# Four edits to the opening of an mLSTM cell with a SwiGLU block: who asks for a load, how a weight block is converted, which engine rounds it, and in what order

## The chip, the cores and the metric

The kernel runs on one core of a Trainium2 chip. The metric is the device time of one execution in microseconds (us), as a median of several runs. The core has a matrix engine (TensorE, PE in the profile; PEld is its weight load), VectorE (DVE), ScalarE (ACT), GpSimd (POOL) and SyncE (SP), which issues transfers. Each engine works through its own list of instructions in order, and semaphores make one wait for another. Transfers (DMAs) are asked for by SP, by ScalarE or by GpSimd.

## The reference

Two stages follow each other. The first is an mLSTM cell over 4 batches, 8 heads, 768 steps and a head size of 40:

```
m_new  = max(f + m, i);  f_stab = exp(f + m - m_new);  i_stab = exp(i - m_new)
C = f_stab * C + i_stab * v k^T;   n = f_stab * n + i_stab * k
y = sigmoid(o) * (C q) / max(|n.q|, 1)
```

Its output, as 3072 tokens of 320 features, goes through a SwiGLU block with d_ff = 1536: `(silu(x @ w_gate) * (x @ w_val)) @ w_out`. The inputs q, k, v and the gates are float32; the three weight matrices are float64 (`np.random.randn` scaled), so that every weight arrives as two 32-bit words.

## The kernel before

The 768 steps are cut into 6 groups of 128. For each group the cell is computed in its parallel form (scores, a matrix of decay weights, a carried state), its result is turned into `xT`, and the 512 tokens of the group go through the SwiGLU block. Group 0 differs from the others: while it runs, the weights are still arriving and have to be turned from float64 into float32 on the chip. The whole change lies in this stretch, up to about 51 us.

**Weights.** The gate and value matrices are cut into 12 blocks of 128 columns (`NFC`), the output matrix into 6 further blocks (numbers 12 to 17). `piece_load` (L166) asks for them in pieces: pieces 0 to 3 are blocks 0 to 3, piece 4 is blocks 4 and 5, piece 5 blocks 6 and 7, and so on. A piece has three parts: part 0, called GATE, is the gate matrix (partitions 0 to 63), parts 1 and 2, called VALUE, are the value matrix (partitions 64 to 127). Part 0 is asked for by SP, parts 1 and 2 by GpSimd (L200).

**Conversion.** A block is converted in three steps. `scale` (L221) has ScalarE make two tiles, `top` from the high words (L226) and `low` from the low words (L228). `join` (L231) has VectorE make the float's bits from `top` (L235, L236). `rounded` (L240) adds `low` as a whole number: on GpSimd, or on VectorE if it is told so (both L243). `top` has one buffer and `low` has two, so the next `scale` waits for the `join` before it. `portion` (L245) scales only some of a block's five chunks of the contraction. Block 0 is converted in two portions, chunks 0 to 1 and 2 to 4; block 1 at once, and both, like block 2, are rounded by VectorE. After that the list `on_vector` (L1041) names the blocks that VectorE rounds: 9 and 10.

**Blocks of group 0.** `hidden(0, m)` (L751) multiplies block m with `xT` in TensorE (L759), ten matmuls into two PSUM banks, which the profile shows as 20 records. The banks come from a ring of four, so block m takes those of block m - 2. Then `first` is run, which converts the block that `ahead` names (block 3 at m = 1, block 4 at m = 2, block 5 at m = 3, ...), and only then follow the SiLU on ScalarE (L764) and the multiplication on VectorE (L765), which release the two banks. After each `hidden`, the entries of `slots` for that m are run.

**Gates of the later groups.** Between the blocks VectorE computes the cell's decay terms for groups 1 to 5. `late_sums` (slot 1) is a running sum of the forget gates (L326) and a subtraction from the input gates (L328), with a memset by GpSimd (L327). `late_maxima` (slot 2) is two small copies (L331, L332) and a running maximum `M_sb` (L333), which GpSimd then stores to memory (`M_store`, L343). From there SP loads it back, broadcast, as `w_sb` (`weights_load`, L515, slot 3). `late_decay` follows in slot 3, the reading of `w_sb` (`weights_cap`, L530) in slot 6.

**The queue of SP around block 0.** SP asks for q, k, v, then for the output gates of the first group (`o_sb`, L139), then for the GATE parts of pieces 0 and 1 (called at L674), 2, 3, 4 and 5. ScalarE's sigmoid of the output gates (L540) comes before the first group's result is turned (`seam`, L507 and the copies at L143) and before block 0 is scaled. GpSimd asks for the VALUE part of piece 0 at L679, between the two calls of `first_values` (L591), multiplies the gates in (`first_gate`, L629) and asks for the other VALUE parts in between.

Of the kernel before, what the change touches and what calls it, by code (L numbers as in the profile page):

```python
# [14 lines left out]
ALU = mybir.AluOpType  # L15
# [9 lines left out]
def kernel(  # L25
# [18 lines left out]
    nc = tc.nc  # L44
# [13 lines left out]
    NKC = DM // HP  # L58
# [15 lines left out]
    def flat(t):  # L74
        return t.rearrange("p c t -> p (c t)")
# [32 lines left out]
    k_sb = const.tile([128, BH, DP], F32)  # L108
# [54 lines left out]

    homes = {}

    def piece_load(p, home=None, parts=(0, 1, 2)):  # L166
        kind, m, n = PIECES[p]
        if kind == "gv":
            a, d = NKC, n * 128
            gate_w, val_w = (w[:, m * 128:(m + n) * 128].rearrange("(c p) f -> p c f", p=HP) for w in (moe_w_gate, moe_w_val))  # L170
            src = [(slice(0, HP), slice(0, NKC), gate_w), (slice(HP, 128), slice(0, NKC - 1), val_w[:, 1:]),
                   (slice(HP, 128), slice(NKC - 1, NKC), val_w[:, 0:1])]
        else:
            a, d = n, DM
            src = [(slice(0, 128), slice(0, n), moe_w_out[m * 128:(m + n) * 128].rearrange("(a p) d -> p a d", p=128))]
        if src[0][2].dtype == F32:
            for r, cs, w in [src[x] for x in parts if x < len(src)]:
                if kind == "o":
                    nc.sync.dma_start(out=wo_sb[r, m:m + n, :], in_=w)
                else:  # L180
                    for x in range(n):
                        nc.sync.dma_start(out=wgv_sb[r, m + x, cs], in_=w[:, :, ts(x, 128)])
            return
        if p in homes:
            raw = homes[p]
        else:
            if p < 4:
                if p == 0:
                    homes["raw"] = conv.tile([128, 4 * NKC * 128], U32, name="raw")
                base = homes["raw"] if p < 2 else raw_h.rearrange("p m t -> p (m t)").bitcast(U32)  # L190
                raw = base[:, ds(2 * (p % 2) * a * d, 2 * a * d)]
            elif home is None:
                raw = conv.tile([128, 4 * NKC * 128], U32, name="raw")
            else:
                raw = home.rearrange("p a t -> p (a t)").bitcast(U32)
            raw = homes[p] = raw[:, 0:2 * a * d]
        for x in parts:
            if x < len(src):
                r, cs, w = src[x]
                eng = nc.gpsimd if x else nc.sync  # L200
                eng.dma_start(out=raw[r].rearrange("p (a d) -> p a d", a=a)[:, cs], in_=w.bitcast(U32))
        words = raw.rearrange("p (a d two) -> p a d two", two=2, a=a)
        raws[p] = (words[:, :, :, 0], words[:, :, :, 1])
        split(p)


    blocks = {}
# [23 lines left out]
    def join(j):  # L231
        if j in blocks:
            lo, top, dst = blocks[j]
            both = dst.bitcast(U32)
            nc.vector.tensor_scalar(both, top, scalar1=3, scalar2=None, op0=ALU.logical_shift_left)  # L235
            nc.vector.scalar_tensor_tensor(both, in0=top, scalar=0x80000000, in1=both, op0=ALU.bitwise_and,  # L236
                                           op1=ALU.bitwise_or)
            blocks[j] = (lo, dst.bitcast(I32))

    def rounded(j, eng=None):  # L240
        if j in blocks:
            lo, dst = blocks.pop(j)
            (eng or nc.gpsimd).tensor_tensor(dst, dst, lo, op=ALU.add)  # L243

    def portion(j, c):  # L245
        if j not in blocks:
            return
        lo, hi, dst = blocks[j]
        if ("room", j) not in homes:
            homes["room", j] = [conv.tile([128, NKC * 128], t, name=n, bufs=x).rearrange("p (a d) -> p a d", a=NKC)  # L250
                                for t, n, x in ((F32, "top", 1), (I32, "low", 2))]
        top, low = homes["room", j]
        nc.scalar.mul(top[:, c], hi[:, c].bitcast(F32), 2.0 ** -112)
        nc.scalar.mul(low[:, c], lo[:, c], 2.0 ** -29)
        blocks[j, c.start] = (low[:, c], top[:, c].bitcast(U32), dst[:, c])

    def convert(j, eng=None):
        scale(j)
        join(j)
        rounded(j, eng)  # L260
# [63 lines left out]

    def late_sums():
        nc.vector.tensor_tensor_scan(flat(f_sb), flat(keep1), flat(f_sb), 0.0, op0=ALU.mult, op1=ALU.add)  # L326
        nc.gpsimd.memset(step1, 0.0)  # L327
        nc.vector.tensor_sub(i_sb, i_sb, f_sb)  # L328

    def late_maxima():  # L330
        nc.vector.tensor_copy(step1[:, 0:1, 0:1], f0[0:BH, end].unsqueeze(1))  # L331
# [258 lines left out]
    def first_values(P):  # L590
        nc.gpsimd.tensor_tensor(vw_sb[:, heads(P)], v_sb[:, heads(P)], w_end[:, heads(P)].to_broadcast([128, UH, D1]),  # L591
                                op=ALU.mult)
# [15 lines left out]
    def first_own(u):  # L608
        both = bank("first_y", "gen")
        spare_of["y", u] = both[:, H * D1:]  # L610
        first_y[u] = both[:, 0:H * D1].rearrange("p (h d) -> p h d", d=D1)
        for h in range(H):
            for i in range(2):
                nc.tensor.matmul(first_y[u][half(i), h, :], lhsT=W0[:, u * H + h, half(i)], rhs=v_sb[:, u * H + h, :],
                                 start=True, stop=True)

    def first_x(u):
        y = first_y.pop(u)
        den = work.tile([128, UH, 1], F32, name="den")[:, 0:H]
        nc.vector.tensor_scalar(den, y[:, :, D:], scalar1=1.0, scalar2=None, op0=ALU.max)  # L620
        nc.vector.scalar_tensor_tensor(den, in0=y[:, :, D:], scalar=-1.0, in1=den, op0=ALU.mult, op1=ALU.max)
        nc.vector.reciprocal(den, den)
        nc.vector.tensor_tensor(x_sb[:, u, 0:DM].rearrange("p (h d) -> p h d", d=D), y[:, :, 0:D],
                                den.to_broadcast([128, H, D]), op=ALU.mult)
# [46 lines left out]
    spread(G, 3, k_sb, 1)  # L671
    first_exp(1)
    first_scores(0)
    for p in range(2):  # L674
        piece_load(p, parts=GATE)
    turn_one(1, q_sb, qT, (A, A), "gen")
    first_ends(1)
    first_values(0)
    piece_load(0, parts=VALUE)  # L679
    first_own(0)  # L680
    turn_one(1, k_sb, kT, (A, A), "gen")
    nc.scalar.activation(warm, warm, AF.Sigmoid)
    first_values(1)
    first_x(0)
    first_own(1)
    first_x(1)
# [25 lines left out]
    join((0, 2))  # L712
    rounded((0, 2), V)
    fill("add", 6, False)
    convert(1, V)
    nc.scalar.activation(warm, warm, AF.Silu)
    first_kept(0, ps0, A)
    first_kept(1, ps1, A)
# [315 lines left out]
    def load_all(dst, a, n, eng=nc.sync):  # L1034
# [3 lines left out]
    run = lambda f, *a, **b: (lambda: f(*a, **b))  # L1038


    on_vector = (9, 10)  # L1041
    ahead = {0: [], 1: [3], 2: [4], 3: [5], 4: [6], 5: [7], 6: [8], 7: [9], 8: [10], 9: [], 10: [], 11: []}
    slots = {
        0: [run(piece_load, 5), run(piece_load, 6, wo_sb)],
        1: [run(late_sums)],
        2: [run(late_maxima), run(M_store, G), run(load_all, k_sb, k, 1)],
        3: [run(late_decay), run(weights_load, 1), run(load_all, q_sb, q, 1)],
        4: [run(nc.scalar.activation, step1, step1, AF.Exp), run(decay_rows), run(cap_table)],
        5: [run(piece_load, 7, parts=GATE), run(load_all, v_sb, v, 1), run(late_turns), run(decay)],
# [132 lines left out]
```

## Time and profile before

| what | value |
|---|---|
| three runs | 507.11, 507.15, 507.64 us; median 507.15 |
| the profiled execution: its own time | 507.54 us |
| its span, first to last instruction | 505.7 us |
| granted TensorE clock | 1.00 over the whole span |
| TensorE busy | 499.6 us (99% of the span) |
| VectorE, ScalarE, GpSimd busy | 335.3, 208.8 and 261.4 us |
| blocks 0 to 5 of group 0 on TensorE (L759) | from 26.89 to 53.69 us |

Times inside the execution count from the start of the span. In a timeline a row gives the start, the length, the engine, the line, the operation, output and input, and in square brackets how long the engine had been idle before it and what ended that. Matmuls overlap: the length of one is longer than its distance to the next, so TensorE's pace is read from the starts. In the chain that ended last, a row gives the start, the length, the engine and the line; it is followed back from the last instruction to whatever released each step. A small q behind an engine's name is its sequencer, and for SP that is its DMA queue.

### The profile page before, as it was taken

To read this page: it belongs to the slowest core of one execution; us is meant where nothing else is said; L and a number is where in the kernel's file an instruction comes from. 1 tells how busy PE (TensorE), PEld (TensorE's weight loads), DVE (VectorE), ACT (ScalarE), POOL (GpSimd) and SP (SyncE) were. 2 spreads that over 40 slices of the span, in tenths; PEclk is the share of its full clock that TensorE was granted. 3 is DMA by queue.
4 is the path that set the end of the run, shared out by engine and by line. 5 is a ranking of instruction groups with operands and counts; after the bars stand their busy time and mean duration, and the time that the engine had idled before them with its cause. 6 is when DMAs were issued, how large, how long until landed. Compare 5 with 4: busy or idle time off the path is not lost.

```text
span 505.7 us, 15057 instructions
## 1 busy us (share of the span) xinstructions
PE 499.6 (99%) x6421; PEld 426.9 (84%) x6421; DVE 335.3 (66%) x543; ACT 208.8 (41%) x407; POOL 261.4 (52%) x293
## 2 busy tenths in 40 slices
PE   8999999999999999999999999999999999999997
PEld 4865555767888899888899888899888899988897
DVE  5779767889998688578376677467568554233421
ACT  4675783467252356323248312339321340223210
POOL 3733534458877834466633367543357650166710
PEclk9999999999999999999999999999999999999999
DMA  9999998697706991502991502992101100000001
GB/s 143 184 254 226 166 231 188 136 181 107 109 7 95 155 96 48 62 3 48 164 131 32 80 5 35 161 133 33 42 3 25 31 2 27 26 1 1 1 14 39
DMA packets 184746, 43.29 MB, mean 86 GB/s; under 512 B 173000, under 2 KB 180184, under 8 KB 184040
## 3 DMA queue, kind: packets, MB, share of 16 engines
q1 hardware_dynamic: 183284, 38.26, 48.2%
q0 software_dynamic: 1264, 4.02, 3.3%
q8 instruction: 50, 0.82, 0.7%
q14 instruction: 16, 0.13, 0.1%
q10 hardware_dynamic: 132, 0.07, 0.0%
HBM read 35.68 MB, written 4.01 MB: 78 GB/s over the span
## 4 chain that ended last, share of the span: by engine, by line
PE 85%; DMA 4%; SPq 4%; DVE 2%; POOL 2%; ACT 2%; issue 1%; POOLq 0%; ACTq 0%; DVEq 0%
PE gv_x L929 26%; PE o_ps L830 21%; PE gv_y L929 21%; PE gv_ps L759 4%; SPq L368 3%; DMA raw<-in_moe_w_gate_dram 3%; PE sp L384 2%; PE o_ps L776 2%; PE inter L433 2%; PE intra L442 1%; DMA w_sb<-M_dram 1%; PE o_ps L835 1%; PE add L410 1%; PE wps L568 1%; PE tp_kq L351 1%
## 5 line engine op out<-in xcount | busy, mean ns | idle before, releaser
L929 PE MATMUL gv_x<-xT,wgv_sb 64*128 64x256 f32 x720 | 89.1, 377 | 0.0
L929 PEld LDWEIGHTS gv_x<-xT,wgv_sb 64*128 64x128 f32 x720 | 69.3, 187 | 8.1 <-issue 0.2
L830 PE MATMUL o_ps<-wo_sb,h_sb 128*128 128x160 f32 x456 | 63.9, 300 | 0.0
L830 PEld LDWEIGHTS o_ps<-wo_sb,h_sb 128*128 128x128 f32 x456 | 62.3, 190 | 1.7 <-issue 1.7
L977 ACT ACTIVATE h_sb<-gv_x 128x256 f32<-128x256 f32 x30 | 11.5, 383 | 116.3 <-PE gv_x L929 116.3
L759 PE MATMUL gv_ps<-xT,wgv_sb 64*128 64x512 f32 x240 | 54.2, 597 | 1.0 <-DVE wgv_sb L243 0.9
L759 PEld LDWEIGHTS gv_ps<-xT,wgv_sb 64*128 64x128 f32 x240 | 28.7, 187 | 21.4 <-issue 14.4
L929 PE MATMUL gv_y<-xT,wgv_sb 64*128 64x256 f32 x360 | 43.9, 376 | 0.0
L929 PE MATMUL gv_y<-q_sb,wgv_sb 64*128 64x256 f32 x360 | 43.9, 376 | 0.0
L395 POOL TENSOR_TENSOR vw_sb<-v_sb,w_sb 128x656 f32<-128x656 f32 x10 | 14.3, 1429 | 50.1 <-ACT w_sb L534 38.1
L929 PEld LDWEIGHTS gv_y<-xT,wgv_sb 64*128 64x128 f32 x360 | 34.9, 187 | 4.0
L929 PEld LDWEIGHTS gv_y<-q_sb,wgv_sb 64*128 64x128 f32 x360 | 34.9, 187 | 4.0
L534 ACT ACTIVATE w_sb<-w_sb,g_T 128x64 f32<-128x64 f32 x128 | 31.0, 333 | 0.0
L929 PE MATMUL gv_x<-q_sb,sw 64*128 64x256 f32 x240 | 30.9, 376 | 0.0
L830 PE MATMUL o_ps<-wT,S 128*128 128x160 f32 x216 | 30.2, 299 | 0.0
L830 PEld LDWEIGHTS o_ps<-wT,S 128*128 128x128 f32 x216 | 29.6, 190 | 0.0
L970 POOL TENSOR_TENSOR tmp<-tmp 128x512 f32<-128x512 f32 x15 | 20.0, 1331 | 16.8 <-DVE tmp L969 16.8
L950 POOL TENSOR_TENSOR h_sb<-x_sb 128x512 f32<-128x512 f32 x12 | 15.7, 1311 | 24.6 <-ACT x_sb L949 24.6
L950 POOL TENSOR_TENSOR h_sb<-tmp 128x512 f32<-128x512 f32 x13 | 16.5, 1268 | 21.5 <-ACT tmp L949 21.5
L776 PE MATMUL o_ps<-wo_sb,h_sb 128*128 128x320 f32 x96 | 27.4, 439 | 0.1
L797 POOL TENSOR_TENSOR S<-h_sb 128x256 f32<-128x256 f32 x30 | 22.6, 754 | 9.4 <-DVE h_sb L950 7.4
L929 PE MATMUL gv_y<-q_sb,sw 64*128 64x256 f32 x200 | 27.0, 388 | 0.0
(234 smaller groups left out, 998.5 us busy)
## 6 DMA issues: line engine op xcount, KB each, us to landing
w_sb<-M_dram SPq DMA_DIRECT2D x10, 512.0 KB, 6.7
v_sb<-in_v_dram SPq DMA_DIRECT2D x12, 320.0 KB, 6.2
o_sb<-in_o_gate_dram SPq DMA_DIRECT2D x12, 320.0 KB, 5.9
raw<-in_moe_w_out_dram SPq DMA_DIRECT2D x3, 1280.0 KB, 6.9
k_sb<-in_k_dram SPq DMA_DIRECT2D x10, 320.0 KB, 7.2
x_sq<-k_sb SPq DMA_DIRECT2D x64, 40.0 KB, 3.2
q_sb<-in_q_dram SPq DMA_DIRECT2D x32, 64.0 KB, 3.7
raw<-in_moe_w_gate_dram SPq DMA_DIRECT2D x3, 640.0 KB
```

The source lines that it names most:

```text
L368: nc.sync.dma_start(out=dst[r, :, t, 0:w], in_=a[:, two:H:2, ds(c * L + t * SQ, SQ), ds(s * SQ, w)].rearrange("b h p d -> p (b h) d"))
L384: nc.tensor.matmul(sp[two][half(i), a, :], lhsT=kT[feats(two), P * UA + a, half(i)], rhs=qT[feats(two), P * UA + a, half(i)], start=True, ...
L395: eng.tensor_tensor(vw_sb[:, heads(P)], v_sb[:, heads(P)], w_sb[:, heads(P), last].to_broadcast([128, UH, D1]), op=ALU.mult)
L534: nc.scalar.activation(w_sb[:, h], w_sb[:, h], AF.Exp, bias=g_T[:, n, h:h + 1], scale=-1.0)
L759: nc.tensor.matmul(ps[i], lhsT=wgv_sb[half(i), m, kc, :], rhs=x[half(i), kc, :], start=(kc == 0), stop=(kc == NKC - 1))
L776: nc.tensor.matmul(ps[u], lhsT=hid(g, m)[:, ts(u, L)], rhs=wo_sb[:, m, :], start=(m == 0), stop=(m == NFC - 1))
L797: eng.tensor_tensor(S1[:, k], lo[:, second_half], hi[:, second_half], op=ALU.add)
L830: nc.tensor.matmul(node[x][:, i], lhsT=lhs(k)[:, ts(i, L)], rhs=rhs(k), start=start and k == 0 and i == 0, stop=stop and k == KH - 1, skip ...
L929: nc.tensor.matmul(ps[:, i, cols], lhsT=lhs(c)[half(i)], rhs=rhs(c)[half(i)], start=start and c == 0, stop=stop and c == n - 1, skip_group ...
L950: (nc.vector if k == KH - 1 else nc.gpsimd).tensor_tensor(h_sb[:, 2 * k + 1], uw[:, 0], uw[:, 1], op=ALU.mult)
L970: nc.gpsimd.tensor_tensor(uw[:, :, second_half], uw[:, :, second_half], uw[:, :, first_half], op=ALU.add)
L977: nc.scalar.activation(h[:, first_half], x[:, 0, first_half], AF.Silu)
```

## The change

- `piece_load` takes an engine to ask with. Block 0's GATE part is no longer asked for by SP after the output gates but by GpSimd, after the second `first_values` and ahead of `first_gate`. Block 1's GATE part takes its place on SP.
- Block 1 is converted in the same two portions as block 0.
- VectorE, not GpSimd, rounds block 4 (`on_vector`).
- Block 5 is no longer converted in `hidden(0, 3)` but at the head of slot 2, ahead of `late_maxima`. Its two scalings keep their place in ScalarE's list. On VectorE its two joins come ahead of the copies, the running maximum and the multiplication of `hidden(0, 3)`; on GpSimd its rounding comes ahead of `M_store`.
- In `late_sums` the subtraction goes from VectorE to GpSimd, ahead of the memset there.

```diff
-    def piece_load(p, home=None, parts=(0, 1, 2)):
+    def piece_load(p, home=None, parts=(0, 1, 2), by=None):
...
-                eng = nc.gpsimd if x else nc.sync
+                eng = by or (nc.gpsimd if x else nc.sync)
...
     def late_sums():
         nc.vector.tensor_tensor_scan(flat(f_sb), flat(keep1), flat(f_sb), 0.0, op0=ALU.mult, op1=ALU.add)
+        nc.gpsimd.tensor_tensor(i_sb, i_sb, f_sb, op=ALU.subtract)
         nc.gpsimd.memset(step1, 0.0)
-        nc.vector.tensor_sub(i_sb, i_sb, f_sb)
...
     first_scores(0)
-    for p in range(2):
-        piece_load(p, parts=GATE)
     turn_one(1, q_sb, qT, (A, A), "gen")
     first_ends(1)
     first_values(0)
     piece_load(0, parts=VALUE)
+    piece_load(1, parts=GATE)
     first_own(0)
     turn_one(1, k_sb, kT, (A, A), "gen")
     nc.scalar.activation(warm, warm, AF.Sigmoid)
     first_values(1)
+    piece_load(0, parts=GATE, by=G)
     first_x(0)
...
-    convert(1, V)
+    for c in (slice(0, 2), slice(2, NKC)):
+        portion(1, c)
+        join((1, c.start))
+        rounded((1, c.start), V)
+    blocks.pop(1, None)
...
-    on_vector = (9, 10)
-    ahead = {0: [], 1: [3], 2: [4], 3: [5], 4: [6], 5: [7], 6: [8], 7: [9], 8: [10], 9: [], 10: [], 11: []}
+    on_vector = (4, 9, 10)
+    ahead = {0: [], 1: [3], 2: [4], 3: [], 4: [6], 5: [7], 6: [8], 7: [9], 8: [10], 9: [], 10: [], 11: []}
...
-        2: [run(late_maxima), run(M_store, G), run(load_all, k_sb, k, 1)],
+        2: [run(convert, 5), run(late_maxima), run(M_store, G), run(load_all, k_sb, k, 1)],
```

## The prediction

> **What bounds the kernel now.** I read the page first, then the chain that ended last, then the engines' timelines between 15 and 62 us.
>
> ```profile
> span 505.7 us, 15057 instructions
> PE 499.6 (99%) x6421; PEld 426.9 (84%) x6421; DVE 335.3 (66%) x543; ACT 208.8 (41%) x407; POOL 261.4 (52%) x293
> ```
>
> TensorE is busy for 499.6 of 505.7 us, so an edit counts only by moving TensorE's start on a block. All edits lie before 51 us. The chain, in order of time, says what holds it there:
>
> ```profile
> 25.00 15.62 DMA raw<-in_moe_w_gate_dram
> ...
> 40.73 0.79 ACT top L226
> ...
> 43.05 1.55 POOL wgv_sb L243
> 44.60 0.04 issue
> 44.64 9.11 PE gv_ps L759 x40
> ```
>
> Block 4's gate weights land at 40.62, ScalarE and VectorE convert them, GpSimd rounds (1.55 us), and TensorE starts block 4 at 44.64. Weight loads (timeline of PEld) show the two waits there:
>
> ```profile
> 44.64 0.30 PEld L759 LDWEIGHTS gv_ps<-xT,wgv_sb 64*128 64x128 f32 x4 [0.92 <-POOL wgv_sb L243]
> 49.19 0.30 PEld L759 LDWEIGHTS gv_ps<-xT,wgv_sb 64*128 64x128 f32 x4 [0.81 <-POOL wgv_sb L243]
> ```
>
> Blocks 4 and 5 both start when GpSimd's rounding ends. Loads come in pairs every 0.43 us, so a block of ten pairs takes 4.29; blocks 0 to 5 would take 25.74 without waits and took 26.80 (26.89 to 53.69). About 1.06 us is lost there: some 0.5 at block 4, 0.15 at block 5, the rest in a slower first pair and the uneven start of block 1. VectorE and GpSimd around it:
>
> ```profile
> 37.39 2.51 DVE L326 TENSOR_TENSOR_SCAN x_sq<-x_sq 32x640 f32<-32x640 f32 x1
> 42.07 0.83 DVE L236 SCALAR_TENSOR_TENSOR wgv_sb<-top,wgv_sb 128x640 uint32<-128x640 uint32 x1
> 42.81 0.68 DVE L765 TENSOR_TENSOR h_sb<-tmp,gv_ps 128x512 f32<-128x512 f32 x1
> 43.48 1.14 DVE L332 COPY x_sq<-x_sq 32x9 f32<-32x9 f32 x1
> 44.66 1.54 DVE L333 TENSOR_TENSOR_SCAN M_sb<-x_sq,M 32x640 f32<-32x640 f32 x1
> ```
>
> ```profile
> 37.03 1.53 POOL L243 TENSOR_TENSOR wgv_sb<-wgv_sb,low 128x640 int32<-128x640 int32 x1 [4.86 <-DVE wgv_sb L236]
> 43.04 1.54 POOL L243 TENSOR_TENSOR wgv_sb<-wgv_sb,low 128x640 int32<-128x640 int32 x1 [2.46 <-DVE wgv_sb L236]
> 46.49 0.64 POOL L343 DMA_DIRECT2D M_dram<-M_sb  x1 [1.90 <-DVE M_sb L333]
> ```
>
> A copy of nine elements takes 1.14 us and ends 0.03 after GpSimd's rounding; a scan that takes 1.54 alone takes 2.51 beside one, 1.34 of it after that ends. So these VectorE operations stand still while GpSimd rounds.
>
> **The change, part by part.**
>
> *Gate half of block 0 by GpSimd.* ScalarE waits for this load at 24.48 (idle 0.41):
>
> ```profile
> 24.48 0.44 ACT L253 ACTIVATE top<-raw 128x256 f32<-128x256 f32 x1 [0.41 <-DMA raw<-in_moe_w_gate_dram]
> ```
>
> On SP it is issued 16.35 to 18.81, queued behind the output-gate loads. On GpSimd it comes after first_values(1), at 17.99, takes about 0.65 to issue (val half: 0.78) and fits into the 1.33 us that GpSimd then idles. The val half landed 4.0 us after its issue, so this lands near 22.5, and SP has one issue of 0.6 less. If nothing else moves, block 0 starts 0.41 sooner, at 26.48. Against it: in the trace's packets the val half (17 to 18 us) left the 160-byte packets of SP's queue 14 KB in that us instead of 165. The last output-gate packets end at 20.46 and ScalarE's second sigmoid starts at 21.39, 0.14 later than instructions there follow each other: it probably waits for them. 320 KB at 209 KB/us push them back by up to 1.5 us. Of that 0.5 is covered (ScalarE's idle 0.52 before the copies at 22.65); the rest delays sigmoid, first_gate(1), its transposes and block 0 by up to 0.6. Bounds -0.41 to +0.6 at block 0's start; I take 0. The Trainium skill (DMA: Bandwidth & Descriptors, "Issuing engines are not separate DMA queues") says that loads of several issuers share the same 16 engines and interleave. By that rule gate half and output gates trade places rather than gain, which is the upper bound again.
>
> *Block 1 in two portions.* ScalarE: 0.34+0.34+0.45+0.47 = 1.60 (steps of block 0's portions) for 1.52. VectorE: 2.71 for 2.16, done near 30.7, before block 1 begins (31.25). Behind it on ScalarE stand the Silu table and first_kept, whose banks block 1's second half takes at 31.41: 0.08 later. That and block 0's shift are hidden at block 4, which waits for its weights: up to about 0.16 of delay costs nothing there.
>
> *The subtraction on GpSimd.* VectorE loses 0.81 at 39.94, then idle until 41.54. GpSimd gets it at 39.96 for about 1.27 (128x640 multiplies: 1.27 to 1.31), and the memset (0.62) ends at 41.87 instead of 40.58. First reader is the copy L331, now after 45. Cost 0 to 0.3: the latter if the memset holds up the shift at 41.54. I take 0; a shift at 53.29 ran its usual 0.47 beside a GpSimd select.
>
> *VectorE rounds block 4.* Landing (40.62), ScalarE and joins stay. Rounding starts 0.96 after L236's start (29.05 to 30.01): 43.03 to 43.86, not 43.04 to 44.59. But hidden(2)'s multiplication stands behind it on VectorE: 43.77 to 44.45 instead of 42.81 to 43.49, and block 4's second bank is block 2's, released by it. TensorE's first matmul can go at 44.0, the second at 44.52 (0.05 to 0.07 after the release, as at 31.41). Before: 44.65. So -0.13, not the -0.5 of the rounding.
>
> *Block 5 ahead of the maxima.* ScalarE has it scaled by 43.79/44.5. Joins 44.37 to 45.73, so GpSimd rounds from 45.87 (0.146 after L236's end, as always here). VectorE goes on with copies and the scan, which would start near 45.88. GpSimd is first by some 0.01: rounding 45.87 to 47.42, scan until 47.42+1.34 = 48.77. Behind the scan stands hidden(3)'s multiplication (0.68, starting 0.08 before its end): 49.37, and its bank is block 5's. Block 5's second half starts at 49.42 instead of 49.20: +0.22. Rounding itself is ready 1.7 us sooner, to no use. If the scan is first, rounding follows it, 47.45 to 49.0, and block 5 starts at 49.05: -0.15.
>
> *The maxima's way.* M_sb is ready at 48.77, not 46.19; its store, also behind the rounding on GpSimd, goes at 49.06 instead of 46.49, and lands 4.7 later by the row above (51.22 before). SP's w_sb loads wait for it, with q, block 10's gate half, v and w_out behind them. The second w_sb landed at 58.45, the cap that reads it ran at 60.60 behind a multiplication that TensorE sets: cover 2.15. Slip 2.57 less the cover and TensorE's own 0.22 leaves 0.2. But the key loads' packets, through which the store went at 48.4 to 50.0, are out by 51.9, so I take some 3.7 for the store and 0 for this term; bounds 0 and +0.2. q (packets until 62, needed at 67.08) and v keep their slack; before piece 9, issued at 76.04, the DMA idles 1.4 us and takes in most of the slip.
>
> Sum: -0.13 at block 4 is overtaken by +0.22 at block 5, which later work hands on (the chain from 53 to 122 us runs through TensorE, and the w_sb load at 99.81 with it): 507.54 + 0.22 = 507.76 against the profiled execution, which lies 0.39 above the median: **507.4**.
>
> The second rule weighed: the Trainium skill (SBUF — State Buffer, "Who interferes with whom") has VectorE and GpSimd share a port pair, held for a whole instruction by whichever issued first. The rows of L326 and L332 agree. By it the 0.01 at 45.87 decides between the last-named starts, so the sum is +0.22 or -0.15.
>
> **The rivals.**
>
> A, the forecast: GpSimd first, 507.4.
>
> B: the scan first, 507.0. For it: 0.01 us is less than I can place. Against: five roundings begin 0.144 to 0.151 after the join.
>
> C, the gain is kept: block 0 goes 0.41 sooner, the weights of block 4 land that much sooner too, because SP's queue has 320 KB less ahead, and the scan doesn't stand in the way. All the loss before 53 us goes: 507.15-1.06 = 506.1. For it: DMA is full throughout. Against: the bytes are the same, and the two bank releases stay.
>
> D, slower: the maxima's store lands late. w_sb's second half comes 7.23 after the store's landing, and beyond 53.5 each us goes into the cap, the exponentials and TensorE's scores at 70 (which waits for ScalarE's qT already). At 4.7 from issue it is +0.2 on top; at 6.3, +1.8: 509.2; the bound of 0.2% is passed at 5.5. For it: weight loads through GpSimd took 4.0 to 13.7 us to land. Against: those had a queue ahead.
>
> **How the numbers follow.** 0.2% is 1.0 us, about what a measurement of this kernel can tell from no change. A 0.33, B 0.2, C 0.2 (three quarters of it past the bound), D 0.27 (nearly all past it, with the memset's 0.3 and block 0's 0.6 adding up). Faster 0.16, same 0.57, slower 0.27. Range: from C, 506.1, to the middle of D, 508.7.
>
> **What would show it.** Right: block 4's first pair spread over 44.0 and 44.5; block 5 released by VectorE's L769, not GpSimd; a scan of about 2.9 us; M_dram stored at 49. Wrong: block 4 before 44.2 (landing moved), a scan of 1.5, VectorE waiting for w_sb near 61, or block 0 away from 26.9 by more than 0.6.

## The result, and the profile after

The changed kernel takes 509.31 us (median of 22 runs, 507.26 to 512.58); the kernel before took 507.13 us (22 runs, 506.10 to 510.06). The ratio is 1.0041, 95% interval 1.0029 to 1.0053: slower by some 0.4%, outside the range that was given. The runs are spread in two clumps that the mean granted clock of TensorE tells apart: in 11 of 22 it is 0.999 or 1.000 and their median is 508.42; in the other 11 it is 0.997 or less and their median is 510.54. So two things have to be found: 1.3 us that are there at full clock, and 2.1 us that come in half of the runs together with a lower clock. In one of the experiments below (e5) two executions took over 1.5% longer than the fastest of their kernel; its ratio leaves them out, and without them its median is 514.31 us instead of 514.72.

The page of the changed kernel (profiled execution 510.32 us, clock 0.997): span, engines, and the rows of TensorE's busy share and clock in 40 slices.

```profile
span 508.5 us, 15066 instructions
...
PE 501.2 (99%) x6421; PEld 425.3 (84%) x6421; DVE 333.7 (66%) x546; ACT 209.5 (41%) x409; POOL 260.6 (51%) x294
...
PE   8989999999999999999999999999999999999997
...
PEclk9989999999999999999999999999999999999999
```

The span is 2.8 us longer, and the third slice (25 to 38 us) has both TensorE's share and its clock a step lower. The chain that ended last now goes through block 0's gate half, between 17 and 28 us:

```profile
17.80 7.82 DMA raw<-in_moe_w_gate_dram
...
25.70 0.44 ACT top L253
...
28.00 2.58 PE gv_ps L763 x7
```

In the timeline, ScalarE waits 1.80 us for it instead of 0.41, and TensorE stands idle for 2.15 us ahead of block 0 instead of 0.87:

```profile
25.70 0.43 ACT L253 ACTIVATE top<-raw 128x256 f32<-128x256 f32 x1 [1.80 <-DMA raw<-in_moe_w_gate_dram]
28.00 3.51 PE L763 MATMUL gv_ps<-xT,wgv_sb 64*128 64x512 f32 x10 [2.15 <-DVE wgv_sb L243]
```

What follows shows in the busy times by windows of 1 us (after the length: each engine's busy share and instructions; the third number from the end is the clock):

```profile
26.00:27.00 1.00, 0.00 (x0) 0.00 (x0) 0.80 (x3) 1.00 (x5) 0.79 (x2) 1.00 1.24 230
27.00:28.00 1.00, 0.00 (x1) 0.03 (x1) 1.00 (x3) 1.00 (x4) 0.00 (x0) 1.00 0.94 201
28.00:29.00 1.00, 1.00 (x6) 0.59 (x8) 0.83 (x3) 0.35 (x2) 0.00 (x0) 1.00 1.00 230
29.00:30.00 1.00, 1.00 (x6) 0.56 (x4) 0.97 (x3) 1.00 (x4) 0.00 (x0) 0.59 1.20 235
30.00:31.00 1.00, 1.00 (x4) 0.40 (x2) 0.83 (x4) 0.98 (x3) 0.26 (x1) 0.50 1.06 222
31.00:32.00 1.00, 1.00 (x4) 0.40 (x2) 0.86 (x2) 0.99 (x3) 1.00 (x3) 0.50 1.02 224
32.00:33.00 1.00, 1.00 (x6) 0.62 (x4) 0.19 (x1) 1.00 (x3) 1.00 (x2) 0.70 1.00 274
```

From about 29.2 to 32.6 the granted clock is 0.50; the two windows that lie wholly in this stretch count four matmuls each, where those of the kernel before count seven or eight. Block 0 lasts 6.06 us (28.00 to 34.06) instead of 4.36. No line of the prediction has this.

Further down, VectorE, GpSimd and the two queues behind them:

```profile
41.33 1.71 POOL L327 TENSOR_TENSOR x_sq<-x_sq 32x640 f32<-32x640 f32 x1 [2.14 <-DVE x_sq L326]
41.68 2.05 DVE L236 SCALAR_TENSOR_TENSOR wgv_sb<-top,wgv_sb 128x640 uint32<-128x640 uint32 x1
...
46.69 1.55 POOL L243 TENSOR_TENSOR wgv_sb<-wgv_sb,low 128x640 int32<-128x640 int32 x1 [3.08 <-DVE x_sq L332]
46.71 2.87 DVE L333 TENSOR_TENSOR_SCAN M_sb<-x_sq,M 32x640 f32<-32x640 f32 x1
49.88 0.65 POOL L343 DMA_DIRECT2D M_dram<-M_sb  x1 [1.64 <-DVE M_sb L333]
...
53.73 5.32 SPq L139 DMA_DIRECT2D q_sb<-in_q_dram  x2
...
61.66 1.17 POOL L201 DMA_DIRECT2D raw<-in_moe_w_val_dram  x2
```

GpSimd was first on block 5 by 0.02 us, and the scan lasts 2.87 instead of 1.54, as forecast. Block 4's join, 0.83 us alone, takes 2.05 beside GpSimd's subtraction. The maxima are stored 3.4 us later than before (46.49). In this execution TensorE is so late itself that none of that stops it before block 10. There ScalarE waits 0.21 us for the value half, asked for at 61.66 instead of 59.46; VectorE's first join of block 10 then takes 1.63 us beside GpSimd's weighting of the values (0.49 before), and blocks 9 to 11 take 0.55 us longer.

The sum over this execution, by the starts of the blocks: +1.11 at block 0 (28.00 against 26.89), +2.81 at block 1, +1.95 at block 6, as blocks 1 to 5 now run without the waits that the kernel before had, +1.97 at block 9, +2.52 at block 11 (84.96 against 82.44), +2.8 at the end.

### The profile page after: what moved, and what is told of

The parts are those of the page before. It is cut to its first block, busy times and chain, and to the rows that moved or that the text cites. A ratio compares the mean times of both kernels' runs of the same rounds, so it can differ in the third digit from the quotient of the medians.

```text
span 508.5 us, 15066 instructions
## 1 busy us (share of the span) xinstructions
PE 501.2 (99%) x6421; PEld 425.3 (84%) x6421; DVE 333.7 (66%) x546; ACT 209.5 (41%) x409; POOL 260.6 (51%) x294
## 4 chain that ended last, share of the span: by engine, by line
PE 93%; DMA 3%; SPq 1%; DVE 1%; POOL 1%; issue 1%; ACT 1%; ACTq 0%; POOLq 0%
PE gv_x L933 26%; PE o_ps L834 21%; PE gv_y L933 21%; PE gv_ps L763 10%; PE o_ps L780 5%; PE inter L433 2%; PE sp L384 2%; PE intra L442 2%; PE add L410 2%; DMA raw<-in_moe_w_gate_dram 2%; PE o_ps L839 1%; DMA h_sb<-in_k_dram 1%; SPq L265 1%; DVE w_sb L519 0%; POOL vw_sb L591 0%
## 5 line engine op out<-in xcount | busy, mean ns | idle before, releaser
L763 PE MATMUL gv_ps<-xT,wgv_sb 64*128 64x512 f32 x240 | 55.7, 610 | 2.1 <-DVE wgv_sb L243 2.1
L763 PEld LDWEIGHTS gv_ps<-xT,wgv_sb 64*128 64x128 f32 x240 | 26.1, 192 | 26.7 <-issue 21.6
L973 DVE TENSOR_TENSOR tmp<-tmp,gv_y 128x1024 f32<-128x1024 f32 x15 | 18.1, 1205 | 13.9 <-PE gv_y L933 12.1
```

Of the source, the lines that this page charges most:

```text
L763: nc.tensor.matmul(ps[i], lhsT=wgv_sb[half(i), m, kc, :], rhs=x[half(i), kc, :], start=(kc == 0), stop=(kc == NKC - 1))
L973: nc.vector.tensor_tensor(uw, uw, y, op=ALU.add)
```

## The experiments

e1, e3 and e4 are edits of the changed kernel, e2 and e7 of the kernel before; for the others it is said at each. All starts below are those of the blocks' first matmuls in one profiled execution each. "0-6", "6-9" and "9-11" are the times between the starts of these blocks; they leave out when block 0 began, which differs by itself from run to run. "Low clock" counts the runs with a mean granted clock of 0.997 or less. Each ratio stands on runs of the kernel before on the same chip (medians 507.13 us for after, 507.78 for e1 to e4, 507.12 for e5 to e8, 508.10 for e9 to e12, 507.72 for e13 to e15). A ratio is not the quotient of the two medians, from which it lies up to 0.13% (0.45% in e5). Of the 113 runs of the kernel before that stand beside e1 to e15, 3 had a low clock.

```
kernel                    ratio, 95% interval        low clock  block 0   0-6    6-9    9-11
before                    1                          3 of 113   26.89    27.89  17.67   9.99
after                     1.0041 [1.0029, 1.0053]    11 of 22   28.00    28.73  17.69  10.54
e1  gate half by SP       1.0047 [1.0024, 1.0071]     4 of 12   27.24    28.27  19.41   9.89
e2  gate half alone       1.0029 [1.0013, 1.0045]     4 of 12   27.56    27.45  17.68   9.86
e3  after, more fill      1.0054 [1.0034, 1.0073]     2 of 6    28.11    27.34  17.68  11.20
e4  gate half early       1.0059 [1.0035, 1.0084]     5 of 8    30.25    28.10  17.68   9.98
e5  e1, q first           1.0097 [1.0060, 1.0135]     6 of 7    26.64    28.21  22.15  11.33
e6  e1, block 5 after     0.9999 [0.9987, 1.0011]     0 of 11   27.03    28.03  17.68   9.86
e7  before, no fill       1.0028 [1.0008, 1.0048]     2 of 12   26.92    27.84  17.68   9.85
e8  e2, more fill         1.0027 [1.0013, 1.0040]     1 of 12   28.07    27.26  17.68   9.86
e9  e6, V rounds 5 too    1.0002 [0.9990, 1.0014]     0 of 12   27.46    27.66  17.67  10.03
e10 block 5 ahead alone   1.0026 [1.0007, 1.0044]     3 of 12   27.64    27.90  19.53   9.85
e11 store late alone      1.0033 [1.0010, 1.0055]     5 of 12   27.26    27.33  22.09   9.86
e12 V rounds 4, 5 alone   0.9980 [0.9968, 0.9992]     0 of 12   27.03    27.42  17.68   9.85
e13 e11, value by SP      1.0077 [1.0051, 1.0104]     2 of 4    27.32    27.38  17.67  15.76
e14 e12 and portions      0.9999 [0.9987, 1.0010]     0 of 12   26.69    27.62  17.68   9.86
e15 e12 and subtraction   1.0003 [0.9990, 1.0016]     0 of 12   27.41    27.83  17.68   9.86
```

The theories at the outset: L, the late load of block 0's gate half and the half clock that follows make the loss; O, the edits of the order make it themselves.

### e1: the gate half by SyncE again

```diff
+    for p in range(2):
+        piece_load(p, parts=GATE)
     turn_one(1, q_sb, qT, (A, A), "gen")
 ...
-    piece_load(1, parts=GATE)
 ...
-    piece_load(0, parts=GATE, by=G)
```

> The changed kernel with the gate half of block 0 asked for by SyncE again, in its old place; the other edits stay. Theory L (the load): nearly all of the loss comes from this half landing 1.2 us later and from the half clock that follows TensorE's 2.15 us of idleness. Then it lands near 24.4, block 0 begins at 26.9, lasts 4.4 us at full clock, and the time is that of the kernel before within 0.6 us: ratio 0.998 to 1.001, with a scan of 2.87 us and block 5 released by VectorE. Rival O (the order edits: GpSimd's subtraction beside the join, the long scan, the later store and value half of block 10) says that they cost the time themselves: ratio 1.003 to 1.005 still.

510.38 us, no faster than the changed kernel. Block 0 begins at 27.24 and lasts 4.36, as L says, but the time is lost again later, and L as it stood has fallen. The chain that ended last, with the scan, the store and what stood behind it on SyncE's queue:

```profile
46.43 2.88 DVE M_sb L333
49.31 0.28 issue
49.60 3.50 DMA M_dram<-M_sb
53.10 0.02 issue
53.11 0.49 SPq L515
...
54.91 15.43 DMA q_sb<-in_q_dram
70.34 0.14 issue
70.48 0.71 PE tp_kq L351 x16
```

The w_sb loads (L515) wait for the stored maxima at the head of SyncE's queue; the two loads of q (L139) stand behind them. Before, they were asked for from 52.41; here from 54.29, and the second lands at 70.34. TensorE begins to turn q at 67.8, and the second half of it waits:

```profile
70.48 0.71 PE L351 MATMUL tp_kq<-x_sq,q_sb 64*128 64x64 f32 x16 [2.00 <-DMA q_sb<-in_q_dram]
```

That is a third theory, Q: the long scan delays the store, the store the loads behind it, and these TensorE. In the changed kernel block 0's delay covers it: there TensorE wants q at 69.0 and q landed at 65.14.

### e2: the gate half alone

```diff
-    for p in range(2):
-        piece_load(p, parts=GATE)
     turn_one(1, q_sb, qT, (A, A), "gen")
 ...
     piece_load(0, parts=VALUE)
+    piece_load(1, parts=GATE)
 ...
     first_values(1)
+    piece_load(0, parts=GATE, by=G)
```

> The kernel before with this one edit: gate half of block 0 by GpSimd after the second multiplication of values, gate half of block 1 by SyncE after block 0's value half. Theory L: landing near 25.6, block 0 at 28.0, granted clock near 0.5 for some 3.5 us after that, block 0 lasting 6.1 us; of these 2.8 us the waits at blocks 4 and 5 (0.65 together) take some back, so +2.0 to +2.8 us, ratio 1.004 to 1.0055. Theory O: block 0's delay is absorbed by the waits at blocks 4 and 5, ratio 1.000 to 1.001.

508.74 us, +0.29%, below the band that L gave and above that of O. The half lands at 25.17, block 0 begins at 27.56. In the profiled run the clock stays full, and the waits at blocks 4 and 5 take most of the delay back (0-6 is 27.45, not 27.89). The eight runs at full clock have a median of 508.42, the four at low clock 510.93.

### e3: TensorE kept busy ahead of block 0

```diff
-    fill("add", 6, False)
+    fill("add", 56, False)
```

> The changed kernel with 56 filling matmuls ahead of block 0 instead of 6, at 0.082 us a pair: TensorE is busy from 25.4 to 27.8 and then goes on to block 0. If idleness drops the clock, block 0 still begins near 28.0 but lasts 4.4 us at clock 1.00, which gives back 1.7 us at block 1; the waits at blocks 4 and 5 then return in part, so the end is 1.0 to 1.7 us sooner than the changed kernel: ratio to the kernel before 1.0005 to 1.002. If the clock falls for another reason (the load it takes on at block 0), block 0 lasts 6.1 us again and the ratio is 1.003 to 1.005.

510.24 us, ratio 1.0054, above both bands. In the profiled run, at clock 1.00, block 0 begins at 28.11 without an idle stretch and lasts 4.32 us, so its clock is whole. What that gave back is lost at blocks 10 and 11 (9-11 is 11.20): ScalarE waits 1.00 us at 72.99 for the gate half of block 10, which stands on SyncE's queue behind q. So Q again, one load further down. Two of six runs still have a low clock, though nothing idles ahead of block 0; where it falls in them is not known.

### e4: the gate half earlier on GpSimd

```diff
+    piece_load(0, parts=GATE, by=G)
     piece_load(0, parts=VALUE)
     piece_load(1, parts=GATE)
 ...
     first_values(1)
-    piece_load(0, parts=GATE, by=G)
```

> The changed kernel with the gate half of block 0 asked for by GpSimd ahead of block 0's value half instead of after the second multiplication of values, issued at some 15.2 instead of 17.8. Theory L, in the form that this queue's descriptors wait for GpSimd's own computing: the packets start by 18 and the half lands between 19.5 and 22; block 0's conversion is then held by ScalarE's own work, it begins at 26.2 to 26.9 at full clock, and the time is 506.3 to 507.3, ratio 0.998 to 1.001. If a load of this queue takes 7.8 us here whatever it meets, it lands near 23, with the same start of block 0. Theory O: ratio 1.003 to 1.005 as before.

510.45 us. The half lands at 19.76, 4.3 us after its issue, yet block 0 begins at 30.25, the latest of all. ScalarE's second sigmoid says why:

```profile
24.66 0.74 ACT L540 ACTIVATE o_sb<-o_sb 128x640 f32<-128x640 f32 x1 [3.16 <-DMA o_sb<-in_o_gate_dram]
```

The output gates, on SyncE's queue, come 3 us later. Here gate half and output gates trade places: the one that goes first makes the other late, and block 0 needs both. TensorE then idles 1.87 us at 24.8 to 26.7, and the windows have half clock from about 25.7 to 32.5:

```profile
25.00:26.00 1.00, 0.00 (x0) 0.00 (x0) 0.49 (x1) 1.00 (x3) 0.52 (x1) 0.85 1.12 219
26.00:27.00 1.00, 0.31 (x6) 0.31 (x8) 0.23 (x1) 1.00 (x5) 1.00 (x2) 0.50 1.11 201
...
32.00:33.00 1.00, 1.00 (x6) 0.53 (x4) 0.97 (x3) 1.00 (x1) 0.75 (x2) 0.74 1.09 243
```

### e5: q ahead of the maxima's readers

```diff
-        3: [run(late_decay), run(weights_load, 1), run(load_all, q_sb, q, 1)],
+        3: [run(late_decay), run(load_all, q_sb, q, 1), run(weights_load, 1)],
```

> The kernel of the run with the gate half by SyncE again, with one more edit: the two loads of q are asked for ahead of the w_sb loads that wait for the stored maxima. Theory Q (the long scan delays the maxima's store, the w_sb loads wait for it at the head of SyncE's queue, and the loads of q behind them land late, so that TensorE waits 2.0 us for q at 68.5): q is issued near 49 to 50, lands by 62, TensorE's transposes of q run in one piece at 67.8, and block 9 begins near 73.2 instead of 74.9; ratio to the kernel before 0.999 to 1.0015 in place of 1.0047. If w_sb is what matters, or the later transfers collide in another way, the ratio stays at 1.003 to 1.005 with another wait between 61 and 75.

On top of e1; 514.72 us, the worst of all, against the expectation of no more than +0.15%. q is there (transposes in one piece at 67.16), but w_sb is now the one behind:

```profile
63.83 2.36 DVE L530 TENSOR_TENSOR w_sb<-w_sb,cap 128x1024 f32<-128x1024 f32 x2 [3.06 <-DMA w_sb<-M_dram]
```

VectorE's cap, and behind it the exponentials, ScalarE's copies of q and TensorE's scores come 3 us late. With the store late, each of the two orders tried has a loser; other orders were not tried.

### e6: block 5 behind the maxima again

```diff
-    ahead = {0: [], 1: [3], 2: [4], 3: [], ...
+    ahead = {0: [], 1: [3], 2: [4], 3: [5], ...
 ...
-        2: [run(convert, 5), run(late_maxima), ...
+        2: [run(late_maxima), ...
```

> The same kernel with block 5's conversion back behind the running maxima; VectorE still rounds block 4, GpSimd still subtracts, block 1 is still in two portions and the gate half is by SyncE. Theory Q: the scan runs alone in 1.5 us, the maxima are stored near 46.5 to 47, q is issued near 53 and is there when TensorE wants it; block 4 starts near 44.2 and block 5 near 49.2; ratio 0.998 to 1.001. If GpSimd's subtraction beside the join, or the portions, cost time of their own, the ratio is 1.002 or more.

On top of e1; 507.38 us, ratio 0.9999, as Q expects, and no run at low clock:

```profile
44.94 1.54 DVE L333 TENSOR_TENSOR_SCAN M_sb<-x_sq,M 32x640 f32<-32x640 f32 x1
...
46.78 0.65 POOL L343 DMA_DIRECT2D M_dram<-M_sb  x1 [4.78 <-DVE M_sb L333]
```

So the loss of e1 (0.47%) is block 5's move, and with both the move and the gate half undone nothing is left of the loss.

### e7 and e8: filling and the clock

Theory H: an idle stretch of TensorE ahead of block 0 brings the half clock, by chance.

```diff
-    fill("add", 6, False)
```

> The kernel before without its six filling matmuls ahead of block 0, everything else as it was: TensorE idles about 1.28 us there instead of 0.87, and block 0 begins at the same time. Theory H (an idle stretch of TensorE of 1 to 2 us brings, by chance of its phase, some 3.4 us at half clock): several of the runs have a mean clock of 0.997 instead of 1.00 and are 1.7 to 2.5 us longer; the median moves by 0 to 1 us. If idleness of that length doesn't matter, no more runs than one in twenty are at 0.997 and the ratio is 0.999 to 1.001.

```diff
-    fill("add", 6, False)
+    fill("add", 36, False)
```

> The kernel with only the gate half by GpSimd, with 36 filling matmuls ahead of block 0 instead of 6 (1.5 us of work in place of 0.25): TensorE's idle stretch there falls under 0.3 us. Theory H: hardly a run at 0.997 (4 of 12 without the filling), and only block 0's later start is left, +0.3 to +0.8 us: ratio 1.0005 to 1.0015. If the clock falls for another reason, a third of the runs are at 0.997 again and the ratio is near 1.003.

e7 is the kernel before without its filling: 508.77 us, +0.28%; 2 of 12 runs have a low clock, where "several" was expected, and the ten others have a median of 508.39, 1.3 above before, for which the one profiled run (507.86 us) shows no reason. Nor does that run test H: TensorE's work ahead of block 0 lasted until 26.90 there, and its longest idle stretch was 0.55 us, not the 1.28 that was expected. e8 is e2 with more filling: 508.37 us, 1 of 12 at low clock instead of 4. But its filling ended at 27.05 and the idle stretch ahead of block 0 was 1.02 us, not the under 0.3 that was expected, so the fewer low clocks can't be put down to it. Neither run settles what brings the low clock (the last section has what the traces say). What e8 shows is that the gate half alone costs time at full clock too: its eleven runs at full clock have a median of 508.30, 1.2 above before. Its trace has half of that (block 0 at 28.07, +1.18, less 0.6 got back in blocks 0 to 6).

### e9 and e12: a version that is faster

```diff
-    on_vector = (4, 9, 10)
+    on_vector = (4, 5, 9, 10)
```

> A version meant to be faster: the kernel with block 5 back behind the running maxima and the gate half by SyncE, in which VectorE rounds block 5 as well as block 4 (0.83 us instead of 1.55). Block 5 can start near 48.7 with its second half near 49.3, released by VectorE's multiplication, instead of 49.48; the maxima's store stays at 46.8. Gain 0.2 to 0.6 us unless the later loads, which stay where they are, take it back: ratio 0.9985 to 1.0005.

```diff
-    on_vector = (9, 10)
+    on_vector = (4, 5, 9, 10)
```

> The kernel before with one edit: VectorE rounds blocks 4 and 5 as well as 9 and 10. Block 4's first pair moves from 44.64 to about 44.2 and 44.6 (its second bank is released by VectorE's multiplication), block 5 starts near 48.8 and 49.3 instead of 49.20, and the maxima are stored as soon as before or 0.5 later. Gain 0 to 0.5 us: ratio 0.9985 to 1.0005. If the store moves by more than that, theory Q gives some of it back.

e9 is that edit on e6: 508.31 us against 508.10, no gain. e12 is the edit on the kernel before, and nothing else: 507.22 us against 508.10, ratio 0.9980, faster than both kernels. In e12 VectorE's roundings take 0.82 us, block 5 starts at 48.56 instead of 49.19, and TensorE hardly waits at blocks 4 and 5 (only the second half of block 5, 0.1 us for VectorE's multiplication):

```profile
42.89 0.82 DVE L243 CUSTOM_DVE_ANT_0 wgv_sb<-wgv_sb,low 128x1280 uint16<-128x1280 uint16 x1
...
47.40 0.82 DVE L243 CUSTOM_DVE_ANT_0 wgv_sb<-wgv_sb,low 128x1280 uint16<-128x1280 uint16 x1
```

0-6 is 27.42 instead of 27.89; with 9-11, 0.6 us less by block 11, where the medians differ by 0.9. The store stays where it was (46.31).

### e10 and e11: block 5's move alone, and the store's lateness alone

```diff
-    ahead = {0: [], 1: [3], 2: [4], 3: [5], ...
+    ahead = {0: [], 1: [3], 2: [4], 3: [], ...
 ...
-        2: [run(late_maxima), ...
+        2: [run(convert, 5), run(late_maxima), ...
```

> The kernel before with one edit: block 5's conversion ahead of the running maxima, GpSimd still rounding block 4. Theory Q: VectorE's joins of block 5 wait for GpSimd's rounding of block 4 to end at 44.6, GpSimd rounds block 5 from about 46.0, the scan lasts 2.9 us and ends near 48.9, the store goes at 49.2 instead of 46.5, and q or w_sb is late for TensorE near 68 to 70: +1.0 to +2.5 us, ratio 1.002 to 1.005, some runs at a clock of 0.997. By the forecast's step (the store's delay is hidden) +0.2: ratio 1.000 to 1.001.

```diff
-        2: [run(late_maxima), run(M_store, G), run(load_all, k_sb, k, 1)],
-        3: [run(late_decay), ...
+        2: [run(late_maxima), run(load_all, k_sb, k, 1)],
+        3: [run(M_store, G), run(late_decay), ...
```

> The kernel before with nothing moved but the maxima's store on GpSimd's queue, from ahead of the rounding of block 5 to behind it: the scan stays at 1.5 us, block 5's rounding starts as soon or sooner, and the store goes near 49.2 instead of 46.5. Theory Q, in which the store's lateness alone costs the time: w_sb and q are issued 1 to 3 us later, TensorE waits for one of them between 66 and 72, +1.0 to +2.5 us, ratio 1.002 to 1.005. If it is the blocked scan or VectorE's order that costs, not the store, ratio 0.999 to 1.001.

e10: 509.12 us, 1.0026; the scan takes 2.87, the store goes at 49.62, TensorE waits 2.12 us for q at 68.5. e11 leaves the scan and VectorE alone and moves only the store behind one rounding: 509.48 us, 1.0033. Its scan, its store and its wait:

```profile
44.48 1.54 DVE L333 TENSOR_TENSOR_SCAN M_sb<-x_sq,M 32x640 f32<-32x640 f32 x1
48.90 0.88 POOL L343 DMA_DIRECT2D M_dram<-M_sb  x1
...
70.60 0.71 PE L351 MATMUL tp_kq<-x_sq,q_sb 64*128 64x64 f32 x16 [3.04 <-DMA q_sb<-in_q_dram]
```

A store 2.4 us later, with nothing else moved, costs as much as the whole move of block 5, and TensorE waits for q as Q says. How often it does so is not shown: of the twelve runs of e11 the seven at full clock go from 507.21 to 509.48, with a median of 508.34 that is only 0.24 above before, and the five at low clock from 511.44 to 512.33; e10 has the same two groups (medians 508.30 and 511.30). The windows of e11 have the clock at 0.50 after that wait, from about 71.3 to 74.7; that makes its 6-9 the 22.09 of the table, where a wait of 2.12 us alone makes 19.5 in e10.

### e13: why q lands ten us after its issue

```diff
-        6: [run(piece_load, 7, parts=VALUE)] + ...
+        6: [run(piece_load, 7, parts=VALUE, by=nc.sync)] + ...
```

> The kernel with only the store late, and with the value half of block 10 asked for by SyncE, behind q and v, instead of by GpSimd at the same time as q's second half. In the run with the late store most of q's 160-byte packets went by 63.5, and the last of them in a trickle beside the value half's packets until 70.4. Theory T (the tail of q loses against the value half of block 10 on the same DMA engines): without that neighbour q is there by 64, TensorE's transposes of q run in one piece near 67, and the wait of 3.0 us is gone; the value half then lands later, near 74 to 76, and block 10 or 11 waits for it instead, so the time may stay at +1 to +3 us: ratio 1.001 to 1.006. If q is late merely because it was asked for late, TensorE still waits for it near 67 to 70.

On top of e11. In the kernel before, q's packets (160 bytes each) are out by 62.1, some 135 KB in a us. In e11 they start before 59 and most are out by 63; from then on, but for one us with 89 KB, 24 KB and less pass in a us, and the load lands only at 70.46. At 62 the packets of block 10's value half begin, which GpSimd asked for at 59.36, while SyncE's issue of q ended at 59.62. With that value half on SyncE, behind v, q's packets pass at 110 to 145 KB in a us until 64, all but 2 KB are out by 65, and TensorE takes q in one piece:

```profile
67.00 1.16 PE L351 MATMUL tp_kq<-x_sq,q_sb 64*128 64x64 f32 x32
```

So it is the collision: q's last packets pass slowly beside the value half's. The Trainium skill (DMA: Bandwidth & Descriptors, "Queues, rings and completion order") has each DMA engine go round between the queues that have work, a whole packet at a time. The trickle of 160-byte packets beside the other queue's larger ones (3.2 KB on average by the totals of the kernel before) agrees with that. The time is 512.27 us, since the value half now lands at 76.63 and block 10 waits 3.2 us for its conversion; the other expectation, mere lateness, is out.

The times of the two issues explain the rest: the issue of q's second load ends 1.7 us before that of the value half begins in the kernel before (57.77, 59.46), 2.6 in the changed kernel (59.05, 61.66; q lands at 65.14), 1.6 in e3 (67.20), and 0.9 or more in every other kernel in which GpSimd asks for the value half and TensorE does not wait for q. In e1, e10 and e11, where TensorE waits, it ends 0.1 to 0.4 us after that.

### e14 and e15: the two edits costed at nothing

```diff
-    convert(1, V)
+    for c in (slice(0, 2), slice(2, NKC)):
+        portion(1, c)
+        join((1, c.start))
+        rounded((1, c.start), V)
+    blocks.pop(1, None)
```

> The kernel in which VectorE rounds blocks 4 and 5 and nothing else is changed (ratio 0.998), and block 1 converted in two portions in addition. With the portions and GpSimd's subtraction the ratio was 1.0002. If the portions cost (ScalarE's copies of the states, which release block 1's second bank, come 0.1 to 0.15 us later): ratio 0.9985 to 1.0005; if they cost nothing: 0.997 to 0.9985.

```diff
+        nc.gpsimd.tensor_tensor(i_sb, i_sb, f_sb, op=ALU.subtract)
         nc.gpsimd.memset(step1, 0.0)
-        nc.vector.tensor_sub(i_sb, i_sb, f_sb)
```

> The kernel in which VectorE rounds blocks 4 and 5 and nothing else is changed (ratio 0.998), and the subtraction of the sums on GpSimd in addition. If the subtraction costs (block 4's join stands beside it for up to 0.5 us, and block 4 and the store come that much later): ratio 0.9985 to 1.0005; if it costs nothing, 0.997 to 0.9985.

Each on top of e12: 0.9999 and 1.0003 in place of 0.9980. By the traces the portions lengthen 0-6 by 0.20 us (27.62), the subtraction by 0.41 (27.83): the first in part through ScalarE's copies of the states, which release block 1's second bank (31.37 after a start at 31.06, where e12 has 31.54 after 31.40), in part at block 5; the second through later joins of block 4. Both edits spend some of what VectorE's rounding gains. The ratios move by more than these 0.2 and 0.4 us; that part lies within the intervals and isn't settled.

## Why the prediction was wrong

*Gate half of block 0 by GpSimd*, taken at 0 with an upper bound of +0.6: mis-sized. The landing was put at 4.0 us after the issue, from the first part of the value half, issued 2.4 us earlier (the second part of that half landed at 20.66, 5.3 us after the half's issue began). Issued at 15.5 (e4) the gate half does land in 4.3 us; issued at 17.8 to 18.2 it took 7.0 to 7.8 and landed at 25.17 to 25.69, later than in every kernel that loads it as before. Block 0 began 1.11 us later, and 0.67 to 1.22 in the other three runs with this load. The forecast let the gate half trade places with the output gates, and e4 shows that trade. In the changed kernel it traded places with block 1's gate half, which the edit puts on SP's queue in its stead: that half landed at 24.18 and block 0's at 25.61, where before block 0's landed at 24.39 and block 1's at 25.88 (e3 and e8 have the new order, e2 has not). Why GpSimd's load moves its first packets only 2.0 to 3.5 us after the issue in these four runs, against 1.6 in e4, is not shown.

*The clock* is a term the sum had not. TensorE's idle stretch of 2.15 us was followed by 3.4 us at half clock and a block 0 that lasted 1.7 us longer, and low clock marks half of the runs, at 2.1 us each.

*Block 5 ahead of the maxima* went as forecast on VectorE and GpSimd, though 0.8 us later: GpSimd first by 0.02 us, a scan of 2.87. In the changed kernel TensorE comes too late to wait there; in e1 VectorE's multiplication releases block 5's second half at 49.94 (49.20 before), and by block 6 e1 is 0.24 us behind e6, which fits the forecast's +0.22. In e10 nothing is left of it by block 6.

*The maxima's way*, taken at 0 with an upper bound of +0.2, is the step that failed with the order edits: "q (packets until 62, needed at 67.08) and v keep their slack". q had 5 us by that count, but a delay of 2 us put its last packets beside the value half of block 10, and they took until 70.4. The store itself landed 2.65 us after its issue in the changed kernel, and 2.5 to 4.4 in the others with a late store and the old order of loads, so the 3.7 that was taken for it was no fault. Rival D had the right side, but by another way: a store that takes over 5.5 us to land, and w_sb late for TensorE. The store was late because it was issued late, and what it made late was q, or in e3 the gate half behind it. e10 puts this step at +0.26% (1.3 us), e1 against e6 at +0.5%.

*VectorE rounds block 4* was right in kind: with block 5 as well it is worth 0.6 us by the trace of e12, where block 4's halves start at 44.27 and 44.52 (44.0 and 44.52 were forecast). In the changed kernel its gain is gone, since TensorE comes late to both blocks. *The subtraction* (0, at most 0.3) costs 0.4 in e15; *the portions* (hidden) 0.2 in e14.

Undoing the gate half alone (e1) wins nothing and undoing both (e6) wins all, because the costs hide one another: the late block 0 asks for block 10's value half 2.2 us later and so keeps it away from q.

The order of the edits' costs is settled by e6, e10, e11 and e13. Open remain: where the clock fell in the runs without a trace, why GpSimd's load starts late, the 1.3 us of e7, and how the 1.3 us of the changed kernel's full-clock runs divide, for which there is no profile of its own (e3, its nearest, has 0.7 at block 6 and 1.2 at blocks 9 to 11).

## What to carry to other kernels

A transfer's slack is not only the distance from its landing to its use, but also the distance to the next large transfer that it would meet if it started later: follow a delayed store through every load queued behind it, and ask which neighbour each of them then has. When a load is put on another queue at a busy place, look for the one that it overtakes and for the one that overtakes it, and take its duration from a load issued at the same time, not from the same load's sibling two us earlier. And count the idle stretch that a change leaves on TensorE: beyond its own length it may cost the clock.

## What the runs showed of the hardware

TensorE's clock. Of the seven profiled executions in which TensorE idled for 1.87 us or more at one of the blocks, five have a granted clock of 0.50 during or after it: with 2.15 us (the changed kernel, for 3.4 us), 1.87 (e4, 6.8 us), 3.04 (e11, 3.4 us), 2.80 (e5, 6.8 us) and 3.2 (e13, 3.4 us); those with 2.00 (e1) and 2.12 (e10) have not. With stretches of up to 1.2 us no profile has it.

The clock records of the traces tell these cases apart. In all seventeen, each stretch of full or half clock between two changes is a whole multiple of 3.413 us (in the changed kernel full clock from 5.29 to 29.18, seven of them, and then one at half clock). If TensorE's idle time is added up over windows of that length, laid so that the changes of the clock fall on their edges, it comes to 2.80 (e5), 2.70 (e11), 2.14 (the changed kernel), 1.86 (e13) and 1.55 us (e4) in the window just ahead of each fall; the matmuls in the rest of e4's window are small ones, of the transposes and the state. e1's 2.00 us were cut by an edge into 0.28 and 1.72, e10's 2.12 into 0.98 and 1.14, and the clock stayed; no other window has over 1.4 us. The edges lie elsewhere in each execution, so what decides, by these traces, is above all how much of an idle stretch falls into one window; that e4 lost the clock with 1.55 and e1 kept it with 1.72 shows that the idle time alone does not settle it. One such window at half clock takes the mean over a span of 508 us to 0.997, two take it to 0.993: that is how the low clocks of the other runs can be read, though where they fell in those is not known.

The Trainium skill (TensorE: Matmul & The Clock Gate, "Part 1: The HAM clock gate") states windows of some 3.4 us that run freely, and half the clock after an idle one. The lengths of 3.4 and 6.8 us, and that stretches of the same length sometimes cost it and sometimes not, agree with free windows; that some 2 us of idleness within a window are enough does not follow from its "≥1 idle window", and here the measurement decides.

Block 0 began between 26.64 and 27.64 in the twelve profiled kernels that load its gate half as before; the half itself landed anywhere from 23.15 (e7) to 25.13 (e10). A change of a few tenths of a us at one block can't be read from one start; the times between blocks can be compared.
